# Normalising attention outputs on GpSimd instead of VectorE, with a planner's constants, table and positions changed

## The chip, the cores and the metric

The kernel runs on one core of a Trainium2 chip. The engines are TensorE (PE, whose weight loads are listed apart as PEld), VectorE (DVE), ScalarE (ACT) and GpSimd (POOL); DMAs are issued from SyncE (SP). The metric is the time of one execution on the device in microseconds, the median over runs; lower is better. The profile records one execution, with every instruction's start and length.

## The reference

A block of a transformer in parallel form: x is 2048 x 512, there are 32 query heads of width 16 that share one key and one value head, and a dense layer with GELU of width 1792.

```python
xn = _layernorm(x)
q = (xn @ wq).reshape(B, S, H, Dh).transpose(0, 2, 1, 3)
k, v = xn @ wk, xn @ wv
p = softmax(einsum("bhqd,bkd->bhqk", q, k) * Dh ** -0.5)
o = einsum("bhqk,bkd->bhqd", p, v)
a = o.transpose(0, 2, 1, 3).reshape(B, S, H * Dh) @ wo
h = gelu(xn @ w1 + b1)
out = x + a + (h @ w2 + b2)
```

## The kernel before

**Tiles.** Queries are cut into 4 blocks of 512, and the heads into 8 groups of 4, so there are 32 passes (`gg`). A pass has 16 key tiles for each of 4 heads, that is 64 score tiles of 128 keys x 512 queries; 2048 in all. Three consecutive tiles make a unit, and there are 683 units. `scores(u)` (L947) issues a unit's matmuls into three banks of PSUM; two sets of three banks take turns, so the scores of unit u + 2 can only start once unit u has been read out of its banks.

**Two ways to an exponential.** A tile goes either to ACT, which computes exp from PSUM into the tile E (`exp`, L970: one instruction for the two or three ACT tiles of a unit), or to DVE. DVE reads the scores from PSUM as integers and writes a piecewise approximation into Dt (`p1`, L1001), and derives three shifted copies of it. Those steps are done for a batch of up to 6 tiles by `close_batch`, following SPL_STEPS: two DVE additions (L1047) make the copies, and then the first buffer itself is shifted in place, one instruction for each tile (L1044). The first buffer before and after its shift and the three copies are multiplied with differently scaled values on PE and summed, five matmuls for a DVE tile (`pv_mm`, L1014), one for an ACT tile. The L1044 steps may run on POOL or on DVE. DTAB is a string with one letter for each unit that says which of its three tiles go to DVE and where a batch ends.

**Normalisation.** The sum of a pass lies in one bank (pO), whose extra row is the softmax denominator. `o_evac(gg)` copies it to Of (L1059), and SP moves numerators and denominators into layout: den, OfP, and, after a reciprocal and a way through DRAM, the broadcast denominators rbP. After each second pass DVE multiplies the two into a slot of oTp:

```python
onorm[gg - h] = onorm[gg] = dve(lambda e: e.tensor_tensor(oTp[0:n, sl, :], OfP[0:n, s, :], rbP[0:n, s, :], ALU.mult), r=keys, ...)   # L1086
```

There are 16 of these, two f32 inputs of 512 columns each and a bf16 result. oTp has 6 slots. `wo_mm` multiplies it with wo (through `mm4`, whose instructions carry L661).

**Side work.** Projections of queries (`q_pack`, `q_m`), the dense layer (`h_mm`, `gelu`, `y_mm`), and the output tiles (`out_tile`) are put at positions counted in units: Q3, QK, HP, YP and GU. They share one bank of PSUM (bank 7, pM). GELU runs on ACT in two stretches, from unit 182 and from unit 512.

**The order.** [...] All instructions are first listed by `add`, with an estimated length (`occ`), a delay until others see the result (`lat`) and an allowance (`allow`); `Prog.schedule` then plays the program through with these, and the order in which it picks becomes the order on each engine. Semaphores enforce real dependences alone. Three rules of it matter here:

- A POOL step of kind `pl` (L1044) is started when DVE picks an instruction that isn't marked `lock` and is at least PL_WIN = 0.4 us long. `lock` marks the DVE steps that don't run beside POOL: L1044, L1047, the squares of the queries and L1086. POOL's step is planned from PL_START (relative to that DVE instruction) for PL_OCC, and lock steps on DVE are held back in the plan until PL_FREE before its end. It gets a semaphore on the last DVE step before the stretch (`gate`).
- A `pl` step that POOL has not taken within PL_TAKE = 1.0 us of being ready may be picked by DVE, and then becomes a DVE step.
- Among ready instructions the one with the smallest ready time plus allowance is picked.

`Prog.settle` replays the final order with another set of delays; from it `emit` sorts the waits of an instruction.

Of the kernel before, what the change touches and what calls it, by code (L numbers as in the profile page):

```python
# [33 lines left out]
S_WAIT = 0.1  # L34
P_WAIT = 0.0
PL_OCC = 0.62
PL_LAT = 0.2
PL_GATE = 0.1
PL_WIN = 0.4
PL_TAKE = 1.0  # L40
PL_DUE = 3.0
PL_START = -0.07
PL_SEM = 0.16
PL_FREE = 0.135
NE_ND_KB = (23, 19, 11, 6)
LA = 34
LB = 120
# [9 lines left out]
DMASK = {".": (), "0": (0,), "2": (2,), "a": (0, 1), "b": (1, 2), "x": (0, 1, 2),  # L57
         "o": (0,), "t": (2,), "A": (0, 1), "B": (1, 2), "X": (0, 1, 2)}
CLOSE = "otABX"
DTAB = "t2t22t00202t..22tt..022.to00.t22t00200..o.t..20222o.o2.tot22.2t.t2222tt22..2o222t2..o202o02tt2.o.2.t0.t202.2.20t0toto.2..0ot.t2..ot0o2t02t.2222o.0t...o0ot2020o2.2t0.02.t00.02.20o002..xxXaoto.02oot.0to2tt.0too0.ot0tot.o0o020t0o0.tt20.t22.o0tto..2t2to220oo.22t0.2ooo.o2t2o.0ot0o.t02t022.to0..oot.2t2t.o0002ot.0.2tto.0tt2.02t0.202t.2t.oo.ot0.00t.t0o0.0o0o..o0o22o2.00.t0tot2.0o2.2o.t2o2o.tt22o.0t.0oo.2ot2t2.o0.t0t20to2.2t0t.tt2t.002tt.oo.o0oooo0.2o0o0.t00t2ot2.0t0tt0.oA.o..020tt2t02..t0000...2o..02ot0020o.t2t...00XbXttto200t.tt0o22tt..0t0t222.o2o2.t2t20.t0t0.t0t00t2o.0tt2tot.t000202t2t.o.0to20.0.2o22t0o.2t00o0t0..t02o0.0o.o0ooto.t2t0to.2oo0o222o0022o00.2t.2..t0t2.2t.tttt2.2.to.o.."  # L60
YF = 664
Y_ALLOW = 8.0
H_ALLOW = 5.0
YT_ALLOW = (3,3,3,3)
WF_ALLOW = 1.5
QP_ALLOW = 1.5
S_LAT = 0.27
S_REAL = 0.222
EXP_OCC = 0.0133
EXP_LAT = 0.16  # L70
Q3 = (7, 4, 2)
QK = ((48,88.7,157.4),(45,107.7,130.4),(62,118.7,159.4))
HP = ((14.33,26.29,49.54,147.27,14,38.77,51.6,14,34.61,92.18,56.17,130.88,103.7,49),(108.69,82.59,66.39,104.08,133,93.7,109.35,162.93,173.36,139,171.29,159.02,133,137.17),(308.62,328.89,290.1,325,306.98,336.81,316.24,310.73,293.91,381.46,369.7,349,374.48,453.6),(475,473.57,427,468.62,459.3,464.72,451,455.66,491.16,486.09,482.33,480.6,464.72,461.37))
YP = ((195.26,184.23,228.93,254.61),(353.39,411.43,387.54,421),(516,530.79,566.23,553.42),(600.53,607,655.32,660.47))
GU = ((182, (0, 1)), (512, (2, 3)))
FG = 7
UB2 = 2
# [25 lines left out]

class _Op:
    __slots__ = ("eng", "fn", "deps", "sdeps", "stream", "amt", "need", "ticket", "waits", "clock", "occ", "lat",
                 "allow", "kind", "tag", "nun", "outs", "rel", "lock", "pm", "rdy", "start", "end", "vis", "idx", "done", "due", "real")


class Prog:
# [16 lines left out]
        self.fill_deps = []  # L126
        self.log = []

    def add(self, eng, fn, r=(), w=(), acc=None, dma=None, occ=0.1, lat=0.15, allow=1.0, kind=None, tag=None, after=(), due=None, lock=False):
        op = _Op()  # L130
        op.lock = lock
        op.eng, op.fn = eng, fn
        op.stream = dma or eng
        op.amt = 16 if dma else 1
        op.need = bool(dma)
        op.ticket = None
        op.occ, op.lat, op.allow, op.kind, op.tag = occ, lat, allow, kind, tag
        op.idx = len(self.ops)
        op.done = False
        op.due = due  # L140
        op.rel = None
        op.pm = any(k == ("bank", 7) or k[0] == ("bank", 7) for k in w)
        deps, sdeps = {}, {}

        def dep(o, raw):
            if o is None or o is op:
                return
            if o.stream == eng == "pe":
                sdeps.setdefault(id(o), (o, False))
                return  # L150
            deps[id(o)] = o
            sdeps[id(o)] = (o, True)

        for k in r:
            dep(self.writer.get(k), True)
            for o in self.accs.get(k, ()):
                dep(o, True)
        for k in w:
            dep(self.writer.get(k), False)
            for o in self.readers.get(k, ()):  # L160
                dep(o, False)
            for o in self.accs.get(k, ()):
                dep(o, False)
        if acc is not None:
            dep(self.writer.get(acc), False)
            for o in self.readers.get(acc, ()):
                dep(o, False)
        op.deps = list(deps.values())
        for o in op.deps:
            o.need = True  # L170
        for k in w:
            self.writer[k] = op
            self.readers[k] = []
            self.accs[k] = []
        for k in r:
            self.readers.setdefault(k, []).append(op)
        if acc is not None:
            self.accs.setdefault(acc, []).append(op)
        for o in after:
            sdeps.setdefault(id(o), (o, True))  # L180
        if self.in_chain:
            o = self.chain.get(eng)
            if o is not None:
                sdeps.setdefault(id(o), (o, False))
            self.chain[eng] = op
        op.sdeps = list(sdeps.values())
        self.ops.append(op)
        return op
# [35 lines left out]
    def schedule(self):  # L224
# [29 lines left out]
                accn[g] = accn.get(g, 0) + 1  # L254
        started = {}
        opened = None
        lockend, gate, prev = 0.0, None, None
        s_seen = False
        vleft = sum(op.kind == "v" for op in ops)
# [6 lines left out]
        while left:  # L266
# [71 lines left out]
            else:  # L338
# [26 lines left out]
                if e == "dve" and op.kind == "pl":  # L365
                    ready["pool"].remove(op)
                    ready["dve"].append(op)
                    op.eng = op.stream = "dve"
                    op.kind, op.occ, op.lat = "post", vcost(TBW, 4), 0.16
                if e == "dve":  # L370
                    if op.lock:
                        gate = prev if prev is not None and t <= prev.end + 0.03 else op
# [49 lines left out]
            if e == "pe":  # L422
                while op.start > wend:
                    slow = 1.0 if area > HAM_T * WIN else 2.0
                    ncold += slow > 1
                    self.log.append((wend - WIN, area / WIN, slow))
                    area, wend = 0.0, wend + WIN
                pend = op.start + op.occ * slow
            free[e] = max(free[e], op.end)
            if op.pm:  # L430
                pmev = op if e == "dve" else None
# [24 lines left out]

    def settle(self):
        free = {e: 0.0 for e, _ in self.SECTIONS}
        mode, cg, pend = None, [0.0] * 4, 0.0
        for op in self.ops:  # L460
            occ = op.occ + EXP_OCC * (op.kind == "exp")
            lat = {"exp": EXP_LAT, "S": S_REAL, "fill": 0.0}.get(op.kind)
            lat = op.lat if lat is None else lat
            t = max([free[op.eng]] + [o.real for o in op.deps])
            if op.eng == "pe":
                if op.kind in ("pv", "side") or (op.kind == "fill" and occ > 0.15):
# [10 lines left out]
                end = t + occ  # L477
            free[op.eng] = max(free[op.eng], end)
            op.real = t + occ + lat

    def emit(self):
        self.settle()
# [44 lines left out]
def bass_parallel_sum__grouped_kv_mqa__dense_activation_gelu__prompt_kernel(  # L527
# [33 lines left out]
    with ExitStack() as es:  # L561
# [78 lines left out]
        def B(b):  # L640
            return ("bank", b)

        def dve(fn, r=(), w=(), n=TBW, mode=1, allow=1.0, lat=0.16, **kw):
            return add("dve", fn, r, w, occ=vcost(n, mode), lat=lat, allow=allow, **kw)

        def act(fn, r=(), w=(), n=TBW, allow=0.0, lat=0.22, **kw):
            return add("act", fn, r, w, occ=0.051 + n / 1.2e3, lat=lat, allow=allow, **kw)
# [1 line left out]
        def mm(o, l, rh, start, stop, r=(), w=(), tp=None, skip=False, occ=0.216, allow=1.5, **ak):  # L649
# [2 lines left out]
                kw["tile_position"] = tp  # L652
            if skip:
                kw["skip_group_check"] = True
            return add("pe", lambda e: e.matmul(o, l, rh, start=start, stop=stop, **kw), r, w, occ=occ, lat=0.23,  # L655
                       allow=allow, **ak)

        def mm4(o, l, rh, start, stop, r=(), w=(), allow=1.5, **ak):
            for j in range(4):
                c = slice(32 * j, 32 * j + 32)  # L660
                add("pe", lambda e, c=c, j=j: e.matmul(o[c, :], l[:, c], rh, start=start, stop=stop,  # L661
                                                       tile_position=(0, 32 * j)),
                    r, [(k, j) for k in w] + [k for k in w if k != B(7)], occ=0.216, lat=0.23, allow=allow, kind="side", tag=(None, j), **ak)

        M4 = [(("bank", 7), j) for j in range(4)]

# [346 lines left out]
        def pv_mm(gg, j, v, kt, rhs, r):  # L1013
            add("pe", lambda e, a, b: e.matmul(pO[32 * j:32 * j + 32, :], V1[:, v, kt, :], rhs, start=a, stop=b,  # L1014
                                               tile_position=(0, 32 * j)),
                r=r + [("V", v, 0 if kt < NVA else NVA)], acc="O", occ=0.216, lat=0.23,
                allow=4.0 if gg < NTB * NGR - 1 or kt < NT - 4 else -5.0, kind="pv", tag=(gg, j))

        def close_batch():
# [18 lines left out]
            for o, i, nb, k in SPL_STEPS:  # L1038
                def keys(b):
                    return [(("D", base[b + m > 0] + q), b + m) for m in range(nb) for q in range(n)]  # L1040
                if o == i:
                    for q in range(n):
                        d = Dt[:, slot(o) + q, :]
                        add("pool", lambda e, d=d, k=k: e.tensor_scalar(d, d, 1.0, float(k), ALU.mult, ALU.add),  # L1044
                            [], [(("D", base[o > 0] + q), o)], occ=PL_OCC, lat=PL_LAT, allow=PL_DUE, kind="pl", lock=True)
                else:
                    dve(lambda e, d=view(o, nb), q=view(i, nb), k=k: e.tensor_scalar(d, q, float(k), None, ALU.add),  # L1047
                        r=keys(i), w=keys(o), n=nb * n * TBW, mode=4, allow=1.0, kind="post", lock=True)
# [8 lines left out]
        def o_evac(gg):  # L1057
# [25 lines left out]
            if h or end:  # L1083
                n = 64 if end else P
                keys = [(k, s, hh, j) for k in ("OfP", "rbP") for hh in range(h + 1) for j in range(HG)]
                onorm[gg - h] = onorm[gg] = dve(lambda e: e.tensor_tensor(oTp[0:n, sl, :], OfP[0:n, s, :], rbP[0:n, s, :], ALU.mult),  # L1086
                                                r=keys, w=[("oTp", sl)] + pre.pop(sl, []), allow=3.0, lock=True)

        def o_norm_last(gg):
            RB1 = [[("rbP", 0, h, j) for j in range(HG)] for h in range(2)]  # L1090
# [81 lines left out]
        def wo_mm(tb, i, ps, start=False, bk=7, al=1.5):  # L1172
            for n, p in enumerate(ps):
# [1 line left out]
                hs = [h for h in range(2) if 2 * pp + h < NTB * NGR - 1]  # L1175
                assert all(2 * pp + h in onorm for h in hs) and 2 * (pp + NPR) + 1 not in onorm
                mm4(bank(bk), oTp[:, pp % NPR, i * P:(i + 1) * P], wop[:, p, :], start and n == 0, False,
                   r=[("oTp", pp % NPR), "wop"], w=[B(bk)], allow=al)

        def b2_mm(bk=7, stop=True, al=1.5):  # L1180
            mm4(bank(bk), ones, b2row[:], False, stop, r=["ones", "b2row"], w=[B(bk)], allow=al)
# [77 lines left out]
        for t in range(NTILE):  # L1259
            if is_d[t]:  # L1260
                first, n = (t, 1) if n == 0 else (first, n + 1)
                if n == KB or last_d[t // TPG] == t or (DTAB[t // 3] in CLOSE and not any(is_d[t + 1:t // 3 * 3 + 3])):
                    bsize[first], n = n, 0

        scores(0)
        scores(1)
        for u in range(NU):
# [89 lines left out]
```

## Time and profile before

| | |
|---|---|
| time, median of 3 runs | 750.98 us (750.9 to 751.15) |
| the profiled execution | 750.71 us, of which its span is 749.0 us |
| PE, DVE, ACT, POOL busy | 732.8, 736.1, 733.2, 364.4 us |
| first and last start of an exponential | 24.1 and 738.6 us |
| normalisations (L1086) | 16, from 101.5 to 737.9 us |
| L1044 steps on POOL and on DVE | 451 and 104 |
| granted TensorE clock | 0.998 |

The span runs from the first instruction to the last; the time holds 1.7 us more around it. Busy time of an engine is the union of its records, and a record ends when the result is written, which is later than the next instruction's start when the engine is pipelined.

### The profile page before, as it was taken

The page shows a single profiled execution, that of the slowest core. Times are in us where ns is not written, and L with a number is a line of the kernel's source. Part 1 is how long each engine was busy: PE and PEld are TensorE (multiplying, and loading weights), DVE is VectorE, ACT ScalarE, POOL GpSimd, SP SyncE. Part 2 cuts the span into 40 slices and gives each one's busy share as a digit, 9 for nine tenths or more (in the row PEclk, how much of TensorE's full clock was granted, in tenths as well). Part 3 has the DMA queues.
Part 4 walks back from the last instruction along what each step waited for, and adds up shares of the span by engine and source line. Part 5 has one row for each costly group of instructions (what it writes and reads, how often), then busy time and mean ns, then how long its engine had stood idle before and what let it go on. Part 6 is the DMA issues. An engine that isn't in the chain of part 4 may idle for free.

```text
span 749.0 us, 21922 instructions
## 1 busy us (share of the span) xinstructions
PE 732.8 (98%) x9046; PEld 228.2 (30%) x9046; DVE 736.1 (98%) x1436; ACT 733.2 (98%) x744; POOL 364.4 (49%) x506
## 2 busy tenths in 40 slices
PE   7999999999999999999999999999999999999998
PEld 4323222222233323232222222332233333322223
DVE  8899999999999999999999999999999999999996
ACT  8999999999999999999999999999999999999995
POOL 5443654343523576554546555553452466454441
PEclk9999999999999999999999999999999999999999
DMA  9200100000011011100101010100100101010101
GB/s 315 61 15 17 32 9 17 24 11 21 6 36 25 9 39 30 24 23 16 26 13 28 17 38 19 29 24 16 25 15 22 40 6 41 23 39 10 25 22 37
DMA packets 32077, 23.34 MB, mean 31 GB/s; under 512 B 16369, under 2 KB 27498, under 8 KB 31978
## 3 DMA queue, kind: packets, MB, share of 16 engines
q1 hardware_dynamic: 30922, 21.90, 10.9%
q8 instruction: 72, 1.18, 0.7%
q14 instruction: 27, 0.22, 0.1%
q10 hardware_dynamic: 1056, 0.03, 0.1%
HBM read 13.08 MB, written 2.35 MB: 21 GB/s over the span
## 4 chain that ended last, share of the span: by engine, by line
PE 40%; DVE 30%; ACT 28%; DMA 0%; issue 0%; SPq 0%
ACT E L970 28%; PE pAll L1014 19%; DVE Dt L1001 13%; PE pAll L947 13%; DVE Dt L1047 10%; PE pAll L661 7%; DVE x_sb L1150 2%; DVE stats L748 1%; DVE Dt L1044 1%; DVE Of L1059 1%; PE pAll L655 1%; DMA x_sb<-in_A_x_dram 0%; DVE oTp L1086 0%; DVE qp L1122 0%; DVE x_sb L1196 0%
## 5 line engine op out<-in xcount | busy, mean ns | idle before, releaser
L970 ACT ACTIVATE E<-pAll 128x1024 bf16<-128x1024 f32 (+1 forms) x678 | 682.4, 1226 | 1.7 <-PE pAll L947 1.2
L1044 POOL TENSOR_SCALAR Dt<-Dt 128x512 int16<-128x512 int16 x451 | 348.2, 772 | 360.6 <-DVE Dt L1047 143.8
L1014 PE MATMUL pAll<-Dt,V 128*32 128x512 bf16 x2775 | 421.8, 383 | 0.6 <-DVE Dt L1047 0.2
L1001 DVE TENSOR_SCALAR Dt<-pAll 128x512 int16<-128x512 f32 (+1 forms) x542 | 364.1, 688 | 1.0 <-PE pAll L947 0.8
L1047 DVE TENSOR_SCALAR Dt<-Dt 128x1024 int16<-128x1024 int16 (+7 forms) x548 | 288.0, 551 | 0.2
L1014 PE MATMUL pAll<-E,V 128*32 128x512 bf16 x1493 | 284.8, 385 | 0.2
L947 PE MATMUL pAll<-QT,KT 32*128 32x512 bf16 x2048 | 267.2, 384 | 6.2 <-ACT E L970 2.1
L947 PEld LDWEIGHTS pAll<-QT,KT 32*128 32x128 bf16 x2048 | 67.3, 91 | 279.5 <-ACT E L970 251.4
L1014 PEld LDWEIGHTS pAll<-Dt,V 128*32 128x32 bf16 x2775 | 110.9, 94 | 119.4 <-issue 72.0
L661 PE MATMUL pAll<-xnT,w_sb 128*32 128x512 bf16 x896 | 122.2, 383 | 0.4 <-DVE x_sb L1150 0.3
L1014 PEld LDWEIGHTS pAll<-E,V 128*32 128x32 bf16 x1493 | 65.9, 94 | 47.5 <-issue 34.7
L661 PE MATMUL pAll<-w_sb,x_sb 128*32 128x512 bf16 x448 | 69.3, 383 | 0.0
L661 PE MATMUL pAll<-w_sb,ub 128*32 128x512 bf16 x448 | 69.3, 383 | 0.0
L661 PE MATMUL pAll<-wop,oTp 128*32 128x512 bf16 x256 | 49.5, 383 | 0.0
L661 PEld LDWEIGHTS pAll<-xnT,w_sb 128*32 128x32 bf16 x896 | 32.1, 95 | 22.4 <-issue 11.8
L1044 DVE TENSOR_SCALAR Dt<-Dt 128x512 int16<-128x512 int16 x104 | 26.7, 279 | 0.0
L661 PE MATMUL pAll<-xnT,wq_sb 128*32 128x512 bf16 x256 | 22.5, 383 | 0.0
L1150 DVE TENSOR_SCALAR x_sb<-pAll,b1T 128x512 bf16<-128x512 f32 x28 | 20.6, 736 | 0.7 <-PE pAll L661 0.6
L1059 DVE COPY Of<-pAll 128x512 f32<-128x512 f32 x31 | 20.9, 674 | 0.0
L1150 DVE TENSOR_SCALAR ub<-pAll,b1T 128x512 bf16<-128x512 f32 x28 | 20.6, 736 | 0.0
L661 PEld LDWEIGHTS pAll<-w_sb,x_sb 128*32 128x32 bf16 x448 | 17.1, 94 | 8.8 <-issue 7.0
L661 PEld LDWEIGHTS pAll<-w_sb,ub 128*32 128x32 bf16 x448 | 17.6, 94 | 4.7 <-issue 2.9
(121 smaller groups left out, 254.6 us busy)
## 6 DMA issues: line engine op xcount, KB each, us to landing
OfP<-Of SPq DMA_DIRECT2D x124, 32.0 KB, 1.9
rbP<-rden_rows SPq DMA_DIRECT2D x124, 32.0 KB, 1.8
w_sb<-in_B_w_dram SPq DMA_DIRECT2D x2, 1792.0 KB, 12.7
x_sb<-in_A_x_dram SPq DMA_DIRECT2D x8, 256.0 KB, 4.3
x_sb<-in_A_x_dram SPq DMA_DIRECT2D x16, 128.0 KB, 2.2
QT<-qp SPq DMA_DIRECT2D x124, 16.0 KB, 1.8
out_dram<-x_sb SPq DMA_DIRECT2D x12, 128.0 KB, 1.7
wq_sb<-in_A_wq_dram SPq DMA_DIRECT2D x1, 512.0 KB, 6.2
```

Source lines behind the costliest of these rows:

```text
L655: return add("pe", lambda e: e.matmul(o, l, rh, start=start, stop=stop, **kw), r, w, occ=occ, lat=0.23, allow=allow, **ak)
L661: add("pe", lambda e, c=c, j=j: e.matmul(o[c, :], l[:, c], rh, start=start, stop=stop, tile_position=(0, 32 * j)), r, [(k, j) for k in w] ...
L748: dve(lambda e, ti=ti, c=c: e.bn_stats(stats[:, c, :], x_sb[:, ti, :]), r=[("x", ti)], w=[("st", ti)], n=511, due=land(ti) + DU["sd"])
L947: ins = e.matmul(o, l, rh, start=True, stop=True, tile_position=(q0, 0))
L970: o = act(lambda e: e.activation(E[:, s0:s0 + na, :], bank(b0, na).rearrange("p (a n) -> p a n", a=na), ACT.Exp, scale=LN2 / 128.0), w=[B( ...
L1001: op = dve(lambda e: e.tensor_scalar(Dt[:, s:s + n, :], bank(bk, n).rearrange("p (a n) -> p a n", a=n), float(127 * 128) + SPL_D, SPL_MIN, ...
L1014: add("pe", lambda e, a, b: e.matmul(pO[32 * j:32 * j + 32, :], V1[:, v, kt, :], rhs, start=a, stop=b, tile_position=(0, 32 * j)), r=r + [ ...
L1044: add("pool", lambda e, d=d, k=k: e.tensor_scalar(d, d, 1.0, float(k), ALU.mult, ALU.add), [], [(("D", base[o > 0] + q), o)], occ=PL_OCC, ...
L1047: dve(lambda e, d=view(o, nb), q=view(i, nb), k=k: e.tensor_scalar(d, q, float(k), None, ALU.add), r=keys(i), w=keys(o), n=nb * n * TBW, m ...
L1059: dve(lambda e: e.tensor_copy(Of[:, i, :], pO), w=["O", ("Of", i)], allow=0.0)
L1150: dve(lambda e: e.tensor_scalar(ubs[tb % 2][:, ft, :], pM, b1T[:, ft:ft + 1], None, ALU.add), r=["b1T"], w=M4 + [ukey(tb, ft)], n=TBW + 57 ...
```

## The change

Five things are changed together.

1. The normalisation becomes two instructions of 256 columns each, listed for POOL as kind `pl`, with ON_OCC as their length. As with L1044, DVE takes one that POOL has not begun in time; its length there is `docc`.
2. `wo_mm` waits, for query tile i, on the half that holds it (i // 2), and on the whole slot for the memset of the last pass.
3. The planner's delays are set to others: PL_LAT, PL_START, PL_FREE, S_LAT, D_LAT, P_LAT, and for ACT a rule in which the end of an instruction depends on the one before it (A_LAG, A_INC, A_SEM). `settle` uses the same delays as `schedule`. The new DVE and PE delays hold from the attention loop on (`dlat`).
4. DTAB is another table. By its letters, 556 tiles instead of 555 go to DVE, in 267 batches instead of 274; of ACT's 678 exponentials 139 instead of 140 have three tiles and 536 instead of 535 have two.
5. The positions HP and YP are others.

```diff
-PL_LAT = 0.2
+ON_OCC = 0.66
+PL_LAT = 0.06
...
-PL_START = -0.07
+PL_START = 0.065
 PL_SEM = 0.16
-PL_FREE = 0.135
+PL_FREE = 0.06
...
-DTAB = "t2t22t00202t..22tt..
...
+DTAB = "t00t00tt.t..o0o0t2tt
...
-S_LAT = 0.27
-S_REAL = 0.222
-EXP_OCC = 0.0133
-EXP_LAT = 0.16
+S_LAT = 0.217
+A_LAG = 0.113
+A_INC = 0.0125
+A_SEM = 0.056
+D_LAT = 0.135
+P_LAT = 0.217
...
-YP = ((195.26,184.23,228.93,254.61),(353.39,411.43,387.54,421),(516,530.79,566.23,553.42),(600.53,607,655.32,660.47))
+YP = ((183.42,183.96,199.68,220),(345.67,404.71,353.43,423.27),(517.64,524.75,562,544),(600,621.42,648.52,662))
...
-                    op.kind, op.occ, op.lat = "post", vcost(TBW, 4), 0.16
+                    op.kind, op.occ, op.lat = "post", op.docc, D_LAT
...
+            if e == "act" and op.kind in ("exp", "gelu"):
+                aend = max(op.end + A_LAG, aend + op.occ + A_INC)
+                op.vis = aend + A_SEM
...
-                onorm[gg - h] = onorm[gg] = dve(lambda e: e.tensor_tensor(oTp[0:n, sl, :], OfP[0:n, s, :], rbP[0:n, s, :], ALU.mult),
-                                                r=keys, w=[("oTp", sl)] + pre.pop(sl, []), allow=3.0, lock=True)
+                first = pre.pop(sl, [])
+                for q in range(2):
+                    c = slice(q * TBW // 2, (q + 1) * TBW // 2)
+                    onorm[gg - h] = onorm[gg] = add(
+                        "pool", lambda e, c=c: e.tensor_tensor(oTp[0:n, sl, c], OfP[0:n, s, c], rbP[0:n, s, c], ALU.mult),
+                        keys, [("oTp", sl, q)] + first, occ=ON_OCC, lat=PL_LAT, allow=PL_DUE, kind="pl", lock=True,
+                        docc=vcost(TBW // 2))
...
-                   r=[("oTp", pp % NPR), "wop"], w=[B(bk)], allow=al)
+                   r=[("oTp", pp % NPR, i // 2), ("oTp", pp % NPR), "wop"], w=[B(bk)], allow=al)
...
+        dlat[:] = D_LAT, P_LAT
```

More of the change, by code (lines that the diff above doesn't have):

```diff
@@ L59 @@
 CLOSE = "otABX"
-DTAB = "t2t22t00202t..22tt..022.to00.t22t00200..o.t..20222o.o2.tot22.2t.t2222tt22..2o222t2..o202o02tt2.o.2.t0.t202.2.20t0toto.2..0ot.t2..ot0o2t02t.2222o.0t...o0ot2020o2.2t0.02.t00.02.20o002..xxXaoto.02oot.0to2tt.0too0.ot0tot.o0o020t0o0.tt20.t22.o0tto..2t2to220oo.22t0.2ooo.o2t2o.0ot0o.t02t022.to0..oot.2t2t.o0002ot.0.2tto.0tt2.02t0.202t.2t.oo.ot0.00t.t0o0.0o0o..o0o22o2.00.t0tot2.0o2.2o.t2o2o.tt22o.0t.0oo.2ot2t2.o0.t0t20to2.2t0t.tt2t.002tt.oo.o0oooo0.2o0o0.t00t2ot2.0t0tt0.oA.o..020tt2t02..t0000...2o..02ot0020o.t2t...00XbXttto200t.tt0o22tt..0t0t222.o2o2.t2t20.t0t0.t0t00t2o.0tt2tot.t000202t2t.o.0to20.0.2o22t0o.2t00o0t0..t02o0.0o.o0ooto.t2t0to.2oo0o222o0022o00.2t.2..t0t2.2t.tttt2.2.to.o.."
+DTAB = "t00t00tt.t..o0o0t2tt0t..o0.o0o02t.22t2.222..0o002o.20t.0o.0o20t.t.2t2t22t22..o.20t00.22t02o.2.t2.222t2.to.22oto2..0t2t2t2..0o22.0o002tt.tt.tt022.t.2.tt2t2ott.tt.00o..2o00.o.t22o0o020.XXx2tt02o.2t0o2ot.02o2.ot0ooo.tot202.0ot0.0t020t..o0.o0t2to.0t200o2o.oo0t0.0t222t2t.o0.t0ot.0t2020.t.t2o.oo000202o.2..o20t..22o0.t2to.0t.0o0000oo0o222..o20.00.0..o00o220.o0ot.2.oo20ooo00oto.o0.t0.0.2ott.00000ooot..202oo..tt2tt.2o0t.o00o2t00.to22.2o20.t.0to020oo.o.02t2t0.0oot.o220t2.t.oo.000020.t2.t.tt.o022.2.t20.2ot000.0ot20.t.axBXtB0oo0o2.2o2o22..202o2ot0.0t2o220.0o02..t2222o0ot.22o.02o2t..2o000oo.2t00t222o02..0tot0o0.2o2.o0.t0to02.tto2t2.to022o..2o2ott20t0222t00..ot0o2...t2tto0o.20.ooot.2t.o.."
 YF = 664
@@ L66 @@
 QP_ALLOW = 1.5
-S_LAT = 0.27
-S_REAL = 0.222
-EXP_OCC = 0.0133
-EXP_LAT = 0.16
+S_LAT = 0.217
[4 more added lines that the diff above has]
+P_LAT = 0.217
 Q3 = (7, 4, 2)
 QK = ((48,88.7,157.4),(45,107.7,130.4),(62,118.7,159.4))
-HP = ((14.33,26.29,49.54,147.27,14,38.77,51.6,14,34.61,92.18,56.17,130.88,103.7,49),(108.69,82.59,66.39,104.08,133,93.7,109.35,162.93,173.36,139,171.29,159.02,133,137.17),(308.62,328.89,290.1,325,306.98,336.81,316.24,310.73,293.91,381.46,369.7,349,374.48,453.6),(475,473.57,427,468.62,459.3,464.72,451,455.66,491.16,486.09,482.33,480.6,464.72,461.37))
-YP = ((195.26,184.23,228.93,254.61),(353.39,411.43,387.54,421),(516,530.79,566.23,553.42),(600.53,607,655.32,660.47))
+HP = ((16,16.66,45.14,142,18.98,83.68,82.91,15.22,41.67,139.91,41.86,124,129.98,72.48),(102.86,77.95,60.89,94,118,148,118,66.17,112,166,165.93,178,144.77,98.2),(298.72,306.87,288.57,322,287.44,286,321.57,310,340,333.65,355.53,334,318.86,474.13),(472,484,448,475.62,460.4,452.61,452.87,475.58,490,493.75,497.47,494.9,450.09,461.11))
+YP = ((183.42,183.96,199.68,220),(345.67,404.71,353.43,423.27),(517.64,524.75,562,544),(600,621.42,648.52,662))
 GU = ((182, (0, 1)), (512, (2, 3)))
@@ L105 @@
     __slots__ = ("eng", "fn", "deps", "sdeps", "stream", "amt", "need", "ticket", "waits", "clock", "occ", "lat",
-                 "allow", "kind", "tag", "nun", "outs", "rel", "lock", "pm", "rdy", "start", "end", "vis", "idx", "done", "due", "real")
+                 "allow", "kind", "tag", "nun", "outs", "rel", "lock", "pm", "rdy", "start", "end", "vis", "idx", "done", "due", "real", "docc")
 class Prog:
@@ L127, in __init__, with add @@
         self.log = []
-    def add(self, eng, fn, r=(), w=(), acc=None, dma=None, occ=0.1, lat=0.15, allow=1.0, kind=None, tag=None, after=(), due=None, lock=False):
+    def add(self, eng, fn, r=(), w=(), acc=None, dma=None, occ=0.1, lat=0.15, allow=1.0, kind=None, tag=None, after=(), due=None, lock=False, docc=0.0):
         op = _Op()
-        op.lock = lock
+        op.lock, op.docc = lock, docc
         op.eng, op.fn = eng, fn
@@ L256, in schedule @@
         opened = None
+        aend = 0.0
         lockend, gate, prev = 0.0, None, None
@@ L458, in settle @@
         free = {e: 0.0 for e, _ in self.SECTIONS}
-        mode, cg, pend = None, [0.0] * 4, 0.0
+        mode, cg, pend, aend = None, [0.0] * 4, 0.0, 0.0
         for op in self.ops:
-            occ = op.occ + EXP_OCC * (op.kind == "exp")
-            lat = {"exp": EXP_LAT, "S": S_REAL, "fill": 0.0}.get(op.kind)
-            lat = op.lat if lat is None else lat
+            occ = op.occ
+            lat = 0.0 if op.kind == "fill" else op.lat
             t = max([free[op.eng]] + [o.real for o in op.deps])
@@ L479, in settle @@
             op.real = t + occ + lat
+            if op.kind in ("exp", "gelu"):
+                aend = max(end + A_LAG, aend + occ + A_INC)
+                op.real = aend + A_SEM
     def emit(self):
@@ L641, in B, with dve @@
             return ("bank", b)
-        def dve(fn, r=(), w=(), n=TBW, mode=1, allow=1.0, lat=0.16, **kw):
-            return add("dve", fn, r, w, occ=vcost(n, mode), lat=lat, allow=allow, **kw)
+        dlat = [0.16, 0.23]
+        def dve(fn, r=(), w=(), n=TBW, mode=1, allow=1.0, **kw):
+            return add("dve", fn, r, w, occ=vcost(n, mode), lat=dlat[0], allow=allow, **kw)
         def act(fn, r=(), w=(), n=TBW, allow=0.0, lat=0.22, **kw):
@@ L654, in mm @@
                 kw["skip_group_check"] = True
-            return add("pe", lambda e: e.matmul(o, l, rh, start=start, stop=stop, **kw), r, w, occ=occ, lat=0.23,
+            return add("pe", lambda e: e.matmul(o, l, rh, start=start, stop=stop, **kw), r, w, occ=occ, lat=dlat[1],
                        allow=allow, **ak)
@@ L662, in mm4 @@
                                                        tile_position=(0, 32 * j)),
-                    r, [(k, j) for k in w] + [k for k in w if k != B(7)], occ=0.216, lat=0.23, allow=allow, kind="side", tag=(None, j), **ak)
+                    r, [(k, j) for k in w] + [k for k in w if k != B(7)], occ=0.216, lat=dlat[1], allow=allow, kind="side", tag=(None, j), **ak)
         M4 = [(("bank", 7), j) for j in range(4)]
@@ L1015, in pv_mm @@
                                                tile_position=(0, 32 * j)),
-                r=r + [("V", v, 0 if kt < NVA else NVA)], acc="O", occ=0.216, lat=0.23,
+                r=r + [("V", v, 0 if kt < NVA else NVA)], acc="O", occ=0.216, lat=dlat[1],
                 allow=4.0 if gg < NTB * NGR - 1 or kt < NT - 4 else -5.0, kind="pv", tag=(gg, j))
@@ L1044, in close_batch @@
                         add("pool", lambda e, d=d, k=k: e.tensor_scalar(d, d, 1.0, float(k), ALU.mult, ALU.add),
-                            [], [(("D", base[o > 0] + q), o)], occ=PL_OCC, lat=PL_LAT, allow=PL_DUE, kind="pl", lock=True)
+                            [], [(("D", base[o > 0] + q), o)], occ=PL_OCC, lat=PL_LAT, allow=PL_DUE, kind="pl", lock=True,
+                            docc=vcost(TBW, 4))
                 else:
```

## The prediction

> **What bounds the kernel now.** I read the page from the top, then the stretches, the chain, the groups and the timeline. First the engines' shares of the span:
>
> ```profile
> PE 732.8 (98%) x9046; PEld 228.2 (30%) x9046; DVE 736.1 (98%) x1436; ACT 733.2 (98%) x744; POOL 364.4 (49%) x506
> ```
>
> Three engines are full and one is half empty. Busy time by stretch (span; then PE, PEld, DVE, ACT, POOL) says that this holds everywhere in the attention loop, not on average only:
>
> ```profile
> 24.00:100.00 76.00, 75.30 (x885) 22.24 (x882) 75.48 (x136) 75.87 (x76) 35.91 (x50) 1.00 0.09 20
> ...
> 290.00:380.00 90.00, 89.15 (x1081) 26.30 (x1078) 89.97 (x178) 89.95 (x90) 47.17 (x65) 1.00 0.09 20
> ...
> 650.00:740.00 90.00, 89.27 (x1127) 26.29 (x1127) 88.47 (x184) 89.71 (x89) 40.98 (x54) 1.00 0.09 22
> ```
>
> DVE is never without work. The page's chain of waits by engine:
>
> ```profile
> PE 40%; DVE 30%; ACT 28%; DMA 0%; issue 0%; SPq 0%
> ```
>
> It changes engine all the time, but two long pieces of it, in the chain in order of time (start, length), lie on the exponentials alone:
>
> ```profile
> 26.70 68.85 ACT E L970 x68
> ...
> 290.77 139.19 ACT E L970 x138
> ```
>
> The groups that the change touches, with the mean ns of one after the busy time:
>
> ```profile
> L970 ACT ACTIVATE E<-pAll 128x1024 bf16<-128x1024 f32 x535 | 519.8, 1139 | 0.8 <-PE pAll L947 0.5
> ...
> L1001 DVE TENSOR_SCALAR Dt<-pAll 128x512 int16<-128x512 f32 x534 | 352.2, 675 | 1.0 <-PE pAll L947 0.8
> L1044 POOL TENSOR_SCALAR Dt<-Dt 128x512 int16<-128x512 int16 x451 | 348.2, 772 | 360.6 <-DVE Dt L1047 143.8 <-PE pAll L1014 93.6 <-DVE Dt L1001 46.2
> ...
> L1044 DVE TENSOR_SCALAR Dt<-Dt 128x512 int16<-128x512 int16 x104 | 26.7, 279 | 0.0
> ...
> L1086 DVE TENSOR_TENSOR oTp<-OfP,rbP 128x512 bf16<-128x512 f32 x15 | 10.1, 676 | 0.0
> ...
> L903 POOL TENSOR_SCALAR V<-oTp 128x256 bf16<-128x256 f32 x5 | 4.3, 866 | 5.9 <-DVE oTp L897 5.5
> ```
>
> The idle column misleads: a record reaches past the start of the next one, so the 0.8 us of idle on the L970 row hides short waits. I therefore count from start to start. The shortest spacing after a two-tile exponential is 0.904 us, after a three-tile one 1.330. From the first exponential's start (24.1) to the last one's (738.6) is 714.5 us; 535 x 0.904 + 140 x 1.330 + 3 x 0.49 + GELU with its table loads 30 make 701.3. So ACT waits 13.2 us. In the piece at 26.70 it waits 0.1 (69 exponentials with the one under way at its end, 54 x 0.904 + 15 x 1.330 = 68.8), in that at 290.77 1.2 of 139.2 (0.85%), but from 641.7 to 738.6 2.5 of 96.9 (2.6%). For DVE the same count gives 706 of the 714.5. ACT and DVE are the bounds, within 1% of each other, and ACT's waits lie where DVE is on the chain. PE has slack in its order, not in its place: it issues scores, sums and side matmuls in one line.
>
> **The change, part by part.** All of it is made against the profiled execution, 750.71 us with 1.7 outside the 749.0 span; the median of the runs is 0.27 above that.
>
> DVE loses 16 normalisations. Each holds DVE 0.600, from the timeline of DVE (start, length):
>
> ```profile
> 100.89 0.68 DVE L1001 TENSOR_SCALAR Dt<-pAll 128x512 int16<-128x512 f32 x1
> 101.49 0.67 DVE L1086 TENSOR_TENSOR oTp<-OfP,rbP 128x512 bf16<-128x512 f32 x1
> 102.09 1.27 DVE L1001 TENSOR_SCALAR Dt<-pAll 128x512 int16<-128x512 f32 x2
> ```
>
> 16 x 0.600 = 9.6 us off an engine that is never idle.
>
> POOL gets 32 halves, 128x256 from two f32 inputs, which no row shows. From below: L1044's unhindered 0.62 (512 columns, one int16 input). From above: L903's 0.866 (256 columns, f32 in). I take 0.70, nearer to L1044, since L903 writes rows of 16 elements apart; 32 x 0.70 = 22.4 us on an engine with 360 idle. The Trainium skill speaks against the move (GPSIMD Engine Reference, "4.1 Engine selection": a two-input elementwise step belongs on VectorE, GpSimd being about twice as slow). By it a half would be an estimated 0.6 and the sum the same; the trace's stretches show why the advice doesn't decide, as POOL is the one engine with room.
>
> Fallback: the planner lets DVE take what POOL hasn't begun within 1 us. Today that is 104 of 555 L1044 steps (19%). As many of the halves make 6, at 256/0.96 ns + 0.067 = 0.333 each: +2.0 (bounds 0 and 32 x 0.333 = 10.7).
>
> Displacement: a half on POOL uses a stretch of DVE's PSUM work that an L1044 could have had, and the L1044 then goes to DVE, at 0.200 start to start. Of 26 halves at one in five: +1.0 (bounds 0 and 5.2).
>
> Port: POOL and DVE's fast int16 steps exclude each other. In the timeline of both:
>
> ```profile
> 93.06 1.32 POOL L1044 TENSOR_SCALAR Dt<-Dt 128x512 int16<-128x512 int16 x2
> ...
> 94.07 0.57 DVE L1047 TENSOR_SCALAR Dt<-Dt 128x1024 int16<-128x1024 int16 x1
> ...
> 94.57 0.67 DVE L1001 TENSOR_SCALAR Dt<-pAll 128x512 int16<-128x512 f32 x1
> ```
>
> POOL is still at it until 94.38 when DVE begins; that step takes 0.57 where its group's mean is 0.414, and the next starts 0.50 later, not 0.33. By the starts of all such pairs (68 in the trace, 2.1 us in all) DVE is held by POOL's remainder less 0.13. POOL mostly begins 0.16 into a 0.60 step, so a half of length L holds DVE L - 0.57: 0.13 at 0.70. For one half in three of 26: +1.1 (bounds: 0 at 0.57, 26 x 0.30 = 7.8 at 0.866).
>
> Tables: one tile more on DVE (556 for 555), 7 batches fewer (267 for 274). The tile: 0.600 + 3 x 0.133 = +1.0; 14 fewer L1047 at their fixed part (278 - 133 - the 76 of overlap = 69 ns): -1.0. Nothing in sum. On ACT one three-tile exponential becomes a two-tile one: -0.43.
>
> The waits: a half in POOL's queue waits for the DMA of rbP and for the DVE step before it, and L1044 steps queue behind it, and the sums of their batch on PE behind those. The DMA has landed: the last rbP issue is 5.0 to 9.5 us ahead of the normalisation now (3.1 for the last), and lands after 1.8. The readers (wo matmuls, from 235.9) are far behind the first normalisation (101.5); only the last one's are close (738.56 to 738.61), and two halves instead of one step there, +0.7 to +1.4, are covered until the final projection at 743.9. SP's queue, DMA and prologue stay. The planner's new latencies and positions change the order of everything: unknown, bounded below under the rivals.
>
> DVE: -9.6 + 2.0 + 1.0 + 1.1 = **-5.5**. Of that, what becomes time? At the 0.85% of the better long piece ACT would wait 6.0 of 701, not 13.2: 7.2 can be had, so 5.5 could in full. But the chain is on DVE for 30% only, and PE's one line stays. I take half, 2.75, plus ACT's 0.43: -3.2. 750.71 - 3.2 + 0.27 = **747.8**.
>
> **The rivals.**
> Whole gain: ACT follows DVE one to one. For it: 0.1 us of waits in the first long piece. Time 750.98 - 5.5 - 0.4 = 745.1; with DVE's full 9.6, capped at 7.2, 743.4.
> No gain: ACT's waits are PE's line, not DVE. For it: PE's 40% of the chain, and scores that start well after their bank is free. Against it: the same line feeds ACT without waits in the long pieces. 750.98 - 0.4 = 750.6, between 749.5 and 752.5.
> Slower, by the port: a half takes 0.87 as L903's row, holds DVE 0.30 each time and pushes one L1044 to DVE. 26 x (0.30 + 0.20) + 2.0 - 9.6 = +5.4; half of it in time and ACT's -0.4 give 753.3, all of it 756. It decides from 0.30 held per half (9.6/32). Against it: only 68 of 451 POOL steps run into DVE at all. The Trainium skill's rule is harsher (SBUF — State Buffer, "Who interferes with whom": whoever starts first has the shared ports for the whole instruction and the other blocks fully). By it, without the 0.13 allowance, a half of 0.70 would hold DVE an estimated 0.26; the trace's pairs agree that it blocks, but not for the last 0.13.
> Slower, by the order: the new positions and latencies leave ACT waiting all along as it does after 641.7. 701 x 2.6% = 18.2, 5.0 more than now; with half of that, 753.1. For it: a plan is only as good as its latencies; against it: nothing in the trace.
>
> **How the numbers follow.** Forecast 0.50 (its own range 745.5 to 749.4), whole gain 0.14, no gain 0.14, port 0.12, order 0.10. About 0.2% (1.5 us) is what a measurement can tell. Faster: 0.50 + 0.14 less 0.01 for the edge; same 0.15; slower 0.22. The range goes from the capped whole gain, 743.4, to the half-converted slow rivals, 753.5; their unconverted ends, some 0.1, and a little below are left out.
>
> **What would show it.** Right: 20 or more of the halves on POOL at 0.6 to 0.75, no DVE row of f32 normalisation above 12 halves, DVE's start-to-start work near 700, ACT's waits near 10, longer pieces of the chain on L970. Wrong: halves above 0.85 or L1047 rows with longer means (port); more than 150 L1044 on DVE (displacement); ACT's waits at 13 with DVE idle (no gain) or above 15 with a full DVE (order).

## The result, and the profile after

The changed kernel takes 748.06 us (median; 747.90 to 748.32), the kernel before 750.94 beside it: a ratio of 0.9962, with an interval of 0.9951 to 0.9972. The forecast was 747.8. The profiled execution took 747.96 with a span of 746.2.

The engines' shares on the page of the changed kernel, and its chain of waits by engine:

```profile
PE 729.0 (98%) x9022; PEld 224.7 (30%) x9022; DVE 732.0 (98%) x1419; ACT 731.3 (98%) x744; POOL 380.6 (51%) x528
...
ACT 76%; PE 14%; DVE 9%; DMA 1%; issue 0%; SPq 0%
```

The shares look as before; the chain doesn't. DVE's part of it went from 30% to 9%, ACT's from 28% to 76%. The same stretches as before (span; then PE, PEld, DVE, ACT, POOL) show no engine freed to the eye, because records overlap:

```profile
24.00:100.00 76.00, 75.44 (x894) 22.55 (x891) 75.28 (x141) 75.22 (x76) 40.28 (x56) 1.00 0.08 19
...
290.00:380.00 90.00, 88.98 (x1051) 26.30 (x1053) 89.55 (x168) 90.00 (x90) 45.49 (x60) 1.00 0.08 20
...
650.00:740.00 90.00, 89.63 (x1160) 26.10 (x1152) 87.26 (x189) 87.13 (x88) 43.02 (x56) 1.00 0.09 23
```

The last stretch is emptier on DVE and ACT since the last exponential in it now starts at 736.0 instead of 738.6. In the chain in order of time the long pieces on the exponentials are now four (start, length):

```profile
26.84 23.33 ACT E L981 x23
...
58.51 145.71 ACT E L981 x143
...
228.40 265.33 ACT E L981 x265
...
571.13 131.03 ACT E L981 x133
```

The groups by form that answer to those of before (count; busy, mean ns of one; idle before). L970, L1001, L1044 and L1086 have become L981, L1012, L1055 and L1102:

```profile
L981 ACT ACTIVATE E<-pAll 128x1024 bf16<-128x1024 f32 x536 | 523.1, 1166 | 1.7 <-PE pAll L958 1.7
L1012 DVE TENSOR_SCALAR Dt<-pAll 128x512 int16<-128x512 f32 x537 | 358.1, 680 | 2.7 <-PE pAll L958 1.6
...
L1055 POOL TENSOR_SCALAR Dt<-Dt 128x512 int16<-128x512 int16 x445 | 340.7, 766 | 323.9 <-DVE Dt L1059 144.0 <-PE pAll L1025 56.3 <-DVE Dt L1012 38.9
...
L1055 DVE TENSOR_SCALAR Dt<-Dt 128x512 int16<-128x512 int16 x111 | 29.5, 282 | 0.0
...
L1102 POOL TENSOR_TENSOR oTp<-OfP,rbP 128x256 bf16<-128x256 f32 x28 | 23.5, 845 | 17.7 <-DVE Dt L1012 8.1 <-DVE Dt L1059 5.4 <-DMA rbP<-rden_rows 1.5
...
L1102 DVE TENSOR_TENSOR oTp<-OfP,rbP 128x256 bf16<-128x256 f32 x2 | 0.8, 415 | 0.0
L1102 DVE TENSOR_TENSOR oTp<-OfP,rbP 64x256 bf16<-64x256 f32 x2 | 0.7, 407 | 0.0
```

28 of the 32 halves ran on POOL and 4 on DVE. The mean of 845 ns on POOL is not the cost of a half: it holds the time for which DVE's fast steps kept POOL out. The instructions of line 1102 (min/median/max ns) say so:

```profile
L1102 POOL TENSOR_TENSOR oTp<-OfP,rbP x28: 718/730/1644, 96.3 to 719.3; 128x256 bf16<-128x256 f32 x28
```

From start to start, as in the prediction, but with one set of spacings for both kernels: DVE's work in the loop fell from 708.5 to 701.8 us (-6.7), the loop from 714.5 to 711.8 (-2.7), ACT's waits from 13.2 to 10.9, and DVE's spare time rose from 6.0 to 10.0.

ACT's own count divides the 2.7 us of the loop: 0.4 is less work, 0.8 less waiting at the exponentials, and 1.5 less waiting in the stretches of GELU. There, in the kernel before, GELU twice waits for the DVE step that writes its input, behind the instructions that start at 218.6 and 563.5, by 0.61 and 0.84 us from start to start. In the view of who waited for whom (us, times, longest) that is this line of the kernel before, and the changed kernel has no such line:

```profile
ACT x_sb L1162 <- DVE x_sb L1150: 1.3, 2, 0.7
```

### The profile page after: what moved, and what is told of

Same layout as the page of the kernel before. It is cut to its first block, busy times and chain, and to the rows that moved or that the text cites. A ratio compares the mean times of both kernels' runs of the same rounds, so it can differ in the third digit from the quotient of the medians.

```text
span 746.2 us, 21865 instructions
## 1 busy us (share of the span) xinstructions
PE 729.0 (98%) x9022; PEld 224.7 (30%) x9022; DVE 732.0 (98%) x1419; ACT 731.3 (98%) x744; POOL 380.6 (51%) x528
## 3 DMA queue, kind: packets, MB, share of 16 engines
q1 hardware_dynamic: 30922, 21.90, 10.9%
## 4 chain that ended last, share of the span: by engine, by line
ACT 76%; PE 14%; DVE 9%; DMA 1%; issue 0%; SPq 0%
ACT E L981 76%; PE pAll L1025 6%; PE pAll L958 4%; PE pAll L672 4%; DVE Dt L1012 3%; DVE Dt L1059 2%; DVE stats L759 1%; DVE x_sb L1167 1%; DMA x_sb<-in_A_x_dram 1%; PE pAll L666 0%; PE pAll L1336 0%; DVE ub L795 0%; ACT xnT L815 0%; ACT ub L792 0%; DVE mv L773 0%
## 5 line engine op out<-in xcount | busy, mean ns | idle before, releaser
L981 ACT ACTIVATE E<-pAll 128x1024 bf16<-128x1024 f32 (+1 forms) x678 | 680.7, 1250 | 2.2 <-PE pAll L958 2.2
L1055 POOL TENSOR_SCALAR Dt<-Dt 128x512 int16<-128x512 int16 x445 | 340.7, 766 | 323.9 <-DVE Dt L1059 144.0
L1012 DVE TENSOR_SCALAR Dt<-pAll 128x512 int16<-128x512 f32 (+1 forms) x544 | 369.2, 692 | 2.7 <-PE pAll L958 1.6
L1025 PE MATMUL pAll<-E,V 128*32 128x512 bf16 x1492 | 281.4, 384 | 0.2 <-DVE Of L1071 0.2
L672 PE MATMUL pAll<-w_sb,x_sb 128*32 128x512 bf16 x448 | 66.7, 383 | 0.0
L672 PE MATMUL pAll<-wop,oTp 128*32 128x512 bf16 x256 | 46.7, 382 | 0.0
L1102 POOL TENSOR_TENSOR oTp<-OfP,rbP 128x256 bf16<-128x256 f32 x28 | 23.5, 845 | 17.7 <-DVE Dt L1012 8.1
L1055 DVE TENSOR_SCALAR Dt<-Dt 128x512 int16<-128x512 int16 x111 | 29.5, 282 | 0.0
```

Of the source, the lines that this page charges most:

```text
L981: o = act(lambda e: e.activation(E[:, s0:s0 + na, :], bank(b0, na).rearrange("p (a n) -> p a n", a=na), ACT.Exp, scale=LN2 / 128.0), w=[B( ...
L1012: op = dve(lambda e: e.tensor_scalar(Dt[:, s:s + n, :], bank(bk, n).rearrange("p (a n) -> p a n", a=n), float(127 * 128) + SPL_D, SPL_MIN, ...
L1102: "pool", lambda e, c=c: e.tensor_tensor(oTp[0:n, sl, c], OfP[0:n, s, c], rbP[0:n, s, c], ALU.mult),
```

## The experiments

Two theories stood against each other. *Room on DVE*: DVE, never idle, set the loop's pace, and work taken off it becomes time in part. *Order*: the gain comes from the new delays, table and positions. The first four runs take the parts of the change singly, the next four keep an order of instructions fixed, and the last four ask how a plan depends on its numbers and whether the bound moved. "Before" beside them stayed between 750.84 and 751.19.

### The parts singly, each with a new plan

**e1**: the changed kernel, normalisation on DVE as before.

```diff
-                for q in range(2):
-                    onorm[gg - h] = onorm[gg] = add("pool", ...halves...)
+                onorm[gg - h] = onorm[gg] = dve(...512 columns...)
```

> The changed kernel with the normalisation put back on DVE as one instruction of 512 columns; constants, table and positions stay the new ones. Theory 'room on DVE': DVE gets some 7 us of work back, its spare time in the loop falls from 10 us to about 4, and the gain goes: 750.3 to 752.0 us, ACT's waits 13 or more. Rival 'order': the gain comes from the new latencies, table and positions, and the normalisation's engine is indifferent: 747.5 to 749.0 us.

Measured: 779.27 us, ratio 1.037 (1.0356 to 1.0384). Neither theory had this.

**e2**: the kernel before, with the halves for POOL and nothing else.

```diff
-                onorm[gg - h] = onorm[gg] = dve(...512 columns...)
+                for q in range(2):
+                    onorm[gg - h] = onorm[gg] = add("pool", ...halves...)
```

> The kernel before with the normalisation in two halves for POOL, and nothing else (old constants, table, positions). Theory 'room on DVE': DVE loses 5 to 7 us of work and half of it shows: 747.5 to 749.3 us. Rival 'order': 750.3 to 751.5 us. If the old plan can't use the room (its table was laid out for a fuller DVE), a time in between.

Measured: 773.87 us, ratio 1.0304 (1.029 to 1.0318).

**e3**: the kernel before, with the new table and positions.

```diff
-DTAB, HP, YP of before
+DTAB, HP, YP of after
```

> The kernel before with the new table and positions only. DVE has as much work as before (one tile more, seven batches fewer). Theory 'room on DVE': 750 to 752.5 us, no gain. Rival 'order': 748 to 749.5 us.

Measured: 784.82 us, ratio 1.0446 (1.0432 to 1.0461).

**e4**: the kernel before, with the new delays.

```diff
-PL_LAT = 0.2    PL_START = -0.07   PL_FREE = 0.135   S_LAT = 0.27  ...
+PL_LAT = 0.06   PL_START = 0.065   PL_FREE = 0.06    S_LAT = 0.217 ...
```

> The kernel before with the new delays of the planner only; normalisation on DVE, old table and positions. Theory 'room on DVE': 750 to 752 us. Rival 'order', in the form that better delays alone order the work better: 748 to 749.5 us.

Measured: 795.26 us, ratio 1.0589 (1.0575 to 1.0604).

Each of the four costs 23 to 44 us, some ten times the gain of the whole, so these runs cannot decide between the theories: each makes a new plan, and that outweighs what was to be told apart. Their profiles show what a plan that doesn't fit looks like. Of e1 (chain by engine; then groups):

```profile
ACT 43%; PE 37%; DVE 18%; issue 1%; DMA 0%; SPq 0%
```

```profile
L1055 POOL TENSOR_SCALAR Dt<-Dt 128x512 int16<-128x512 int16 x380 | 287.8, 757 | 449.2 <-DVE Dt L1059 178.6 <-PE pAll L1025 110.6 <-DVE Dt L1055 53.2
...
L1055 DVE TENSOR_SCALAR Dt<-Dt 128x512 int16<-128x512 int16 x176 | 44.5, 283 | 0.0
```

POOL takes 380 of the shifts instead of 445 and DVE 176 instead of 111, 13 us of work more on DVE. By the count from start to start DVE's work in e1's loop is some 21 us above the changed kernel's and its spare time some 11 us longer, so the loss is work and waiting. (That DVE, once late in the plan, leaves POOL fewer stretches and so gets still more of the shifts is a likely reading, which no run isolates.) Who waited for whom in e1 (us, times, longest) has the exponentials waiting whole microseconds for PE; in the same view of the changed kernel none waits longer than 0.5:

```profile
ACT E L981 <- PE pAll L1025: 21.2, 11, 4.1
```

and in e3 GELU waits for the dense layer, whose tiles come too late for their position:

```profile
ACT x_sb L1162 <- DVE x_sb L1150: 15.2, 3, 7.8
...
ACT ub L1162 <- DVE ub L1150: 7.5, 1, 7.5
```

### The same edits at a fixed order

Here the program is planned as it was, and instructions are changed only afterwards, so that order and positions stay.

**f1**: the kernel before; DVE's normalisations are shortened, which takes work off DVE and puts none on POOL.

```diff
-dve(lambda e: e.tensor_tensor(oTp[0:n, sl, :], OfP[0:n, s, :], rbP[0:n, s, :], ALU.mult), ...)
+m = TBW if gg < 12 else 16
+dve(lambda e: e.tensor_tensor(oTp[0:n, sl, 0:m], OfP[0:n, s, 0:m], rbP[0:n, s, 0:m], ALU.mult), ...)   # planned as before
```

> The kernel before with its order of instructions untouched on every engine; from the seventh normalisation on, DVE multiplies 16 columns of 512 (the rest of the slot keeps older values). That takes 10 x 0.52 = 5.2 us off DVE and nothing else. Theory 'room on DVE' (about half of it becomes time): 748.4, between 747.0 and 749.6 us. Rival 'order' (the plan alone sets the time, and DVE's room is idle): 750.5 to 751.5 us. If DVE decides alone: 745.8 us.

Measured: 749.90 us, ratio 0.9986 (0.9977 to 0.9995). Faster, but 1.1 us of 5.2 (DVE's work by the same count: 708.5 to 703.4), a fifth, less than the theory's half: the time lies between the ranges of the two theories. GELU's two waits are still there (0.61 and 0.68 us).

**f2**: the kernel before; after planning, normalisations go to POOL in halves.

```diff
+for op, halves in norms:       # after schedule(), before emit()
+    pr.to_pool(op, halves)     # ahead of the next DVE step of 0.5 us or more that isn't `lock` and has no POOL step beside it
```

> The kernel before with its order untouched, except that 15 normalisations are cut in halves after planning and 25 of the 30 halves are put into POOL's order at stretches that the plan leaves free (5 halves and the last normalisation stay on DVE). DVE loses 9.0 - 5 x 0.333 = 7.3 us. Theory 'room on DVE': half shows, 747.3, between 745.5 and 749.3 us. Rival 'order': 750.5 us or more. If POOL's halves hold DVE as long as they free it: 750 to 753 us.

Measured: 749.78 us, ratio 0.9984 (0.9975 to 0.9993): 1.2 us of 7.3, again between the ranges. The chain, and the halves:

```profile
ACT 44%; PE 37%; DVE 17%; DMA 1%; issue 0%; SPq 0%
```

```profile
L1136 POOL TENSOR_TENSOR oTp<-OfP,rbP 128x256 bf16<-128x256 f32 x25 | 18.3, 732 | 20.1 <-DVE Dt L1096 13.4 <-DVE Dt L1050 3.6 <-DVE Dt L1093 1.4
```

At a fixed order the move to POOL is a gain by itself, e2's loss notwithstanding. A half that isn't blocked takes 0.73 us. Seven of the 25 were still at work when a fast int16 step of DVE began, and the starts of the steps behind show DVE held by 0.9 us in all; of the 6.4 that are left, 1.2 is a fifth, as in f1. GELU's two waits stay here too (0.61 and 0.69 us).

**f3**: the changed kernel; its POOL halves are executed by DVE.

```diff
+for op in norms:               # after schedule(), before emit()
+    if op.eng == "pool":
+        op.eng = op.stream = "dve"
```

> The changed kernel with its order untouched, except that the 28 halves planned for POOL are executed by DVE at the same place: 28 x 0.333 = 9.3 us of work more on DVE, whose spare time in the loop is 10.2. Theory 'room on DVE': 752.5, between 750.5 and 757 us. Rival 'order': 747.5 to 749 us.

Measured: 753.87 us, ratio to before 1.0039 (1.0027 to 1.0052); 5.8 us above the changed kernel for 9.3 us of work, within the theory's range and far outside the rival's. GELU's two waits are absent as in the changed kernel; what grows is ACT's waiting at the exponentials, by 5.9 us. The halves stand where POOL was to do them, so f3 prices this order with DVE in POOL's place, not the best order for DVE. The chain is again shared, as in the kernel before:

```profile
PE 37%; ACT 34%; DVE 27%; issue 1%; DMA 0%; SPq 0%; DVEq 0%
```

**f4**: the changed kernel; the halves on POOL are shortened.

```diff
-"pool", lambda e, c=c: e.tensor_tensor(...)
+"pool", lambda e, c=(c if gg < 12 else slice(q * TBW // 2, q * TBW // 2 + 8)): e.tensor_tensor(...)
```

> The changed kernel with its order untouched; from the seventh normalisation on a half on POOL multiplies 8 columns of 256 (the rest keeps older values), so that POOL's part of the cost is nearly gone. Theory: POOL is off the path and its halves hold DVE by 1 us in all: 747.3 to 748.3 us. Rival 'port' (the halves hold DVE, the gain would be larger without): under 747 us.

Measured: 748.03 us (747.90 to 748.29), as the changed kernel. The cut reaches the 18 later halves on POOL and the last two, which run on DVE. That POOL's part costs nothing at DVE the trace of the changed kernel shows for all 28: only four were still at work when a fast int16 step of DVE began, with 0.06 to 0.09 us left, and the DVE step behind started at its usual spacing each time.

Four times make the account: the order of before with normalisation on DVE 750.97, on POOL 749.78; the order of after with it on DVE 753.87, on POOL 748.06. The new order without the room is 2.9 us *slower* than the old one; with the room it is 1.7 faster than the old order with most of it. The room alone is worth 1.2 us (f2); this order is worth something only with the room.

### Numbers of the plan, and the bound

**g1**: the changed kernel, with a half planned at its true length.

```diff
-ON_OCC = 0.66
+ON_OCC = 0.73
```

> The changed kernel with one constant other: a half of the normalisation is planned at 0.73 us, the length that its trace shows, instead of 0.66. If a plan is good because its numbers are near to the chip's, the time stays or falls: 747.3 to 748.6 us. If table and positions are fitted to one plan to the letter, as the four runs with parts of the change suggest, any other number throws the plan off: 755 to 785 us, with DVE taking 130 or more of the L1055 steps instead of 111.

Measured: 767.49 us, ratio 1.0222 (1.0208 to 1.0236), with 161 shifts on DVE. A number nearer to the chip's makes the kernel 19 us slower, because it makes another plan.

**g2**: the changed kernel with the old delays (the reverse of e4's diff).

> The changed kernel with the old delays of the planner; halves on POOL, new table and positions. If the parts are fitted to each other: 765 to 790 us. If the delays were a matter of indifference and only the halves with their table count: 747.5 to 749.5 us.

Measured: 790.16 us, ratio 1.0521 (1.0506 to 1.0535). With g1 this makes six new plans, each 17 to 44 us slower than before, and each with 161 to 185 shifts on DVE; that table and positions fit one plan only is shown for these six. What the new delays are worth to a table laid out for them, and whether they are worth more than others would be, stays open: that needs a table fitted to each, which was not tried.

**g3** and **g4**: the kernel after and the kernel before, with 12 exponentials cut at a fixed order.

```diff
-o = act(lambda e: e.activation(E[:, s0:s0 + na, :], bank(b0, na)...
+m = 2 if na == 3 and u >= 60 and three[0] % 10 == 0 else na     # three[0] counts the three-tile ones
+o = act(lambda e: e.activation(E[:, s0:s0 + m, :], bank(b0, m)...
```

> The changed kernel with its order untouched; 12 of its 139 three-tile exponentials, one in ten from unit 60 on, compute two tiles only (the third keeps older values). That takes 12 x 0.426 = 5.1 us off ACT and nothing else. Theory 'the change moved the bound from DVE to ACT' (chain 76% on ACT): 60 to 80% of it becomes time, 743.9 to 745.2 us. Rival (DVE binds as before): 747.0 us or more.

> The same cut of 12 exponentials in the kernel before, its order untouched: 5.1 us off ACT. Theory (DVE and PE's line carry 70% of the chain before, ACT 28%): 20 to 40% of it becomes time, 748.9 to 750.0 us. Rival (ACT was the bound in both): 746.0 to 747.5 us.

Measured: 745.76 after (2.3 us of 5.1 become time, 45%) and 750.34 before (0.5 of 5.1, 10%, its interval of 0.9984 to 1.0001 reaching no change). Both lie below what was expected, but the contrast stands: ACT's time was nearly worthless before and is worth almost half of itself now. The chain of g3 and that of g4 go with it: with ACT shortened, PE's part rises from 14% to 35% in the one, and ACT's stays at 28% in the other.

```profile
ACT 50%; PE 35%; DVE 13%; DMA 1%; issue 0%; SPq 0%
```

```profile
PE 35%; DVE 35%; ACT 28%; issue 1%; DMA 1%; SPq 0%
```

## Why the prediction was right, point by point

- **DVE's relief**: -5.5 forecast, -6.7 measured. But the count from start to start takes one spacing for each kind of step and so can't hold the port's +1.1; without it the forecast is -6.6, and the parts came out nearly as added up. Halves on DVE: 4 instead of 6 (+1.3 us). Displacement: 111 shifts on DVE for 104, one of them for the additional tile (7 x 0.2 = +1.4, forecast +1.0). Table: about nothing, as worked out.
- **Port**: the term of the sum that was mis-sized. +1.1 was taken, for halves of 0.70 us. They take 0.73, and still f4, which nearly removes them from the seventh normalisation on, changes nothing, and the trace shows no delay of DVE behind any of the 28: the term is 0. One half in three running into a DVE step was too many (four of 28 did), and these had under 0.1 us left: the plan holds those steps back until near POOL's end. In f2, where the steps were planned without the halves, it is 0.9. All fast DVE steps that found POOL at work were held 1.4 us in all, against 2.1 before.
- **Waits in POOL's queue**: as forecast. Only one shift on POOL waited for a half, for 1.0 us (in the instructions of line 1102).
- **What becomes time**: "half" gave the right number by luck and was a guess about the wrong thing. Half of 6.7 and ACT's 0.4 is 3.8; measured were 2.9, and the port's +1.1, which wasn't there, brought the sum near. And the share isn't one figure of the kernel: it is a fifth at the old order and six tenths at the new one, and the gain is a difference, +2.9 for the order and -5.8 for the room. GELU's 1.5 us belong to the order: f3 gets them without the room, f1 and f2 don't get them with it. Which part of the new order removes those waits no run isolates.
- **Bound**: ACT's waits were to fall to about 10 and the chain to lie on L970 (now L981) in longer pieces; 10.9, and 76%, though of this fall only 0.8 us lie at the exponentials. g3 and g4 confirm by intervention that the bound moved, by less than the chain's shares said.
- **Rivals**: *no gain* falls with f1 to f3. *Port* falls with f4. *Whole gain* was not reached: 2.9 us of 7.1, and 5.8 of 9.3 at the new order (f3). That PE's line takes the rest fits g3's chain and isn't shown. *Order* was misjudged in kind: priced at 753 as a drift of ACT's waits, it is 2.9 us for this order without its room and 17 to 44 us for plans that don't fit. The forecast treated a new order as a small unknown, which the new table and positions happened to make true. Its row was misread, too: the 2.5 us of waits from 641.7 on leave the exponential out that is under way there. From that one's start, at 641.46, ACT waits 1.4 of 97.2 us (1.5%), which over 701 us is 10.3 and less than the 13.2 it waited; the row gave no reason for a loss.
- **The Trainium skill**: its advice to keep two-input steps on VectorE (GPSIMD Engine Reference, "4.1 Engine selection") agrees in kind: two halves cost POOL 1.46 us against DVE's 0.60, 2.4 times. The prediction's estimate of 0.6 for a half would not have left its sum the same: its own rule makes 0.3 of the port's 1.1 then, and -6.3 in all. The advice doesn't decide where VectorE is full and GpSimd half idle, as f3 against the changed kernel shows.

## What to carry to other kernels

Between three engines at 98%, read the chain and spacings from start to start rather than busy shares: they pointed to where relief pays, and a cut on the engine (f1, g3, g4) measures how much of it becomes time, here less than the chain's share (45% for 76%, 10% for 28%). Where an order is planned with estimated numbers and its positions are fitted to the plan, never judge one part of a change by planning anew; fix the order, change the instruction, and compare. And a planner's constant nearer to the hardware is no improvement by itself: with table and positions left as they were it cost 19 us here (g1). Fitting them to it again was not tried.

## What the runs showed of the hardware

- The normalisation on GpSimd, 256 columns of two f32 inputs and a bf16 result, takes 0.73 us (718 to 737 ns where DVE didn't keep it out), between L1044's 0.62 for 512 int16 columns and L903's 0.866. The halves of 8 columns in f4 take 0.20 where nothing keeps them out (197 to 206 ns, 10 of 18), so that it is about 0.18 fixed and 2.1 ns for each column: (727 - 201) / 248. Their group (busy, mean ns of one) shows how far a mean on POOL can be from the cost, since eight of the 18 were kept out:

```profile
L1102 POOL TENSOR_TENSOR oTp<-OfP,rbP 128x8 bf16<-128x8 f32 x18 | 6.6, 378 | 16.6 <-DVE Dt L1012 8.2 <-DVE Dt L1059 4.3 <-DMA rbP<-rden_rows 1.5
```
